# One plan for the whole recurrence and its tail, with constant matmuls in TensorE's gaps

## The chip, the cores and the metric

The kernel runs on one core of a Trainium2 chip. The metric is device time in microseconds of one execution, taken on the chip.

## What is computed

A linear-attention recurrence over 768 steps for 4 batches of 8 heads, with states of 40 x 40, then a mixture of 8 experts with a skip rule over the 3072 resulting rows of 320. Everything is float32.

```python
for t in range(S):
    y[:, :, t] = np.einsum('bhd,bhde->bhe', rt, state)
    Sa = np.einsum('bhde,bhe->bhd', state, at)
    state_decay = state * wt[:, :, None, :] - np.einsum('bhd,bhe->bhde', Sa, bt)
    state = state_decay + np.einsum('bhd,bhe->bhde', vt, kt)
...
do_compute = x @ w_skip > 0              # x: rows of y, 320 wide
e_idx = np.argmax(xc @ w_gate, axis=1)   # xc: the rows that compute
h = np.maximum(xc[mask] @ w1[e], 0.0)
y[mask] = gate_w[mask, None] * (h @ w2[e])
out[do_compute] = xc + y
```

## The kernel before

**The recurrence.** The 768 steps are cut into 24 chunks of 32 steps; heads and batches lie in 16 groups, and each chunk is worked in two halves `w` of 8 groups. A half passes through a chain: `ux` (TensorE product, pc<-R1t,L1t; a copy to UX), `uq` (product with the inverted triangle TB, four copies to R1t, and a mask product R1t<-R1t,mc, on GpSimd in all chunks but the last), `sst` (the state products, ps<-R1t,L2t, whose result goes to the next chunk's R1t and to YT). Every second chunk has `rs` (pc<-rrt,SS). Beside the chain stand work that prepares later chunks (`scan_z`, `scan_w`, `kbm`, `l1a`, `m1`, `kbt`, `m2`) and `tinv`, a long series of small VectorE products that inverts the triangle of four chunks at a time. `yt` turns a finished chunk, stores it and makes the scores; `route` picks each row's expert, ranks the rows with small matmuls by constants (pq<-oh,mc) and scatters them with GpSimd's indirect DMAs to the DRAM table xg.

**The order.** `Rec` records the calls of the engines as tasks instead of emitting them. `deps` finds what depends on what, `plan` is a list scheduler with fixed costs per operation (`cost`), a model of how TensorE's program is fetched, and PSUM banks that it hands out: PQ (1), PC (3) and PS (2), where a tile of the state products takes a PS bank only and PX (2) lies outside the plan. A task's priority is its place in the program less the length of the work that follows it (`up`). ScalarE's copies out of PSUM may go to VectorE where that starts more than `ALT` earlier. `flush` emits the tasks in planned order, so every recorded instruction carries line 255 in the profile, and one emitted directly carries line 129.

**The tail.** `flush` is called at the start of chunk 22. The tile M, which held work space of the earlier chunks, is then released, and its memory becomes WH0 and WL0, the high and low parts of expert 0's weights (made from WR by `split`: five casts and five subtractions, all on VectorE for expert 0), and a small tile ex. Chunks 22 and 23, the routing of the last rows and the following sums run in program order: `xacc` multiplies the rows already scattered for expert 0 (loaded back from xg by `early`) by the identity into PSUM, and `xadd` adds the rows of the last two chunks by one-hot matrices, so that expert 0 starts without waiting for their scatter. `warm(k)` puts k matmuls of constants (128 x 512) before some of these steps.

**The experts.** Eight experts follow, each with two layers of three products of split (fp32r) operands, weights loaded and split one expert ahead.

Of the kernel before, what the change touches and what calls it, by code (L numbers as in the profile page):

```python
# [43 lines left out]
class Task:  # L44
    __slots__=("e","op","calls","R","W","d","lat","out","p","n","pr","al","up","k","v","x","g")
class Eng:
# [15 lines left out]
class Rec:  # L62
# [4 lines left out]
    def __init__(s,nc):  # L67
        s.nc=nc; s.on=False; s.ni=0; s.tasks=[]; s.own={}; s.na=0; s.first={}; s.cache={}; s.banks={}; s.rest=()
        n=s.shim=Shim(); n.nc=nc
        for k,e in s.ENG.items(): setattr(n,k,Eng(s,e,getattr(nc,k)))  # L70
# [57 lines left out]
    def call(s,e,op,fn,a,k):  # L128
# [6 lines left out]
        r=[y for x in list(a[1:])+[v for n,v in k.items() if n!='accum_out'] for y in ap(x)]  # L135
        W=[u for x in w for u in s.use(x)]; R=[u for x in r for u in s.use(x)]
        d,lat=s.cost(e,op,w,r,a)
        own=dict(s.own)
        L=s.tasks[-1] if s.tasks else None
# [6 lines left out]
        t.x=s.pipe(w[0],r[0]) if op=='dma_start' else 0.0  # L146
        t.v=s.cost('V','copy',w,r,a)[0] if e=='A' and op=='copy' and 'PSUM' in str(r[0].space).upper() and W[0][0][0]=='s' else None
        s.tasks.append(t)
    def deps(s):
        acc={}  # L150
        for t in s.tasks: t.p,t.n,t.al=set(),[],set()
        for i,t in enumerate(s.tasks):
            for wr,L in ((0,t.R),(1,t.W)):
                u={}
                for n,q,m in L: u[n,q]=u.get((n,q),0)|m
                for (n,q),m in u.items():
                    if n[0]=='v': t.al.add(n[1])
                    h=acc.setdefault(n,[])
                    for j,w2,q2,m2 in h:
                        if j!=i and ((wr or w2) and q&q2 and m&m2 or n[0] in ('v','px') and s.tasks[j].e!=t.e and (n[0]!='v' or 'P' in (s.tasks[j].e,t.e))): t.p.add(j)  # L160
                    if wr and n[0] in 'sd': h[:]=[x for x in h if not (x[0]!=i and x[2]|q==q and x[3]|m==m)]
                    h.append((i,wr,q,m))
        for i,t in enumerate(s.tasks):
            for j in t.p: s.tasks[j].n.append(i)
        for t in reversed(s.tasks):
            t.up=t.d*s.PW+max([s.tasks[j].up+t.lat+t.x+(s.HOP if s.tasks[j].e!=t.e else 0) for j in t.n],default=0)
    def plan(s,keep=False):
# [8 lines left out]
        def put(i):  # L176
            pool[T[i].e].append(i)
            if T[i].v and not keep and s.ALT<9: pool['V'].append(i)
        for i in range(N):
            if not left[i]: put(i)  # L180
        nxt={e:0 for e in 'VAGPS'}; seq={e:[i for i in range(N) if T[i].e==e] for e in 'VAGPS'}
        def want(i):

            got={}; t0=0.0
            while old and old[0] in bank: old.pop(0)
# [9 lines left out]
        done=0; old=sorted(users); lv=lg=0.0  # L195
        while done<N:
            best=None
            for e in 'VAGPS':
# [6 lines left out]
                c.sort(key=lambda x:s.key[x[1]])  # L205
                x=c[0]; du=lambda i: T[i].v if e!=T[i].e else T[i].d
# [4 lines left out]
                if best is None or x[0]+(s.ALT if e!=T[x[1]].e else 0)<best[0]+(s.ALT if best[3]!=T[best[1]].e else 0): best=x+(e,)  # L211
# [4 lines left out]
            en[i]=e; st[i]=t0; fin[i]=t0+(t.v if e!=t.e else t.d)  # L216
            if e=='P':
# [21 lines left out]
        s.st,s.fin,s.bank_of,s.en,s.span=st,fin,bank,en,max(fin)  # L239
    LET=1.0; FAR=1.0; ALT=1.0; FILL=None  # L240
    def keys(s):
# [3 lines left out]
    def flush(s):  # L245
        s.on=False
        s.deps(); s.keys(); s.plan()
        def at(x,own):
            if isinstance(x,bass.AP) and x.name in s.banks:
                return bass.AP(s.banks[s.bank_of[own[x.name]]].tensor,x.offset,[tuple(d) for d in x.ap])  # L250
            return x
        work=[(s.st[i],i) for i in range(len(s.tasks))]+(s.fill() if s.FILL else [])
        for _,i in sorted(work,key=lambda x:x[0]):
            if isinstance(i,tuple): s.FILL(*i); continue
            for fn,a,k,own in s.tasks[i].calls: (fn if s.en[i]==s.tasks[i].e else s.nc.vector.tensor_copy)(*[at(x,own) for x in a],**{n:at(x,own) for n,x in k.items()})  # L255
        s.tasks=[]
    def fill(s):

        life={}
        for i,t in enumerate(s.tasks):  # L260
            for o in t.al:
                a,b=life.get(o,(1e9,0)); life[o]=(min(a,s.st[i]),max(b,s.fin[i]))
        P=sorted((s.st[i],s.fin[i]) for i in range(len(s.tasks)) if s.en[i]=='P')
        r=[]
        for (_,a),(b,_) in zip(P,P[1:]):
            if b-a<0.6: continue
            for n in s.banks:
                if all(e<a-0.3 or f>=b for o,(f,e) in life.items() if s.bank_of[o]==n):
                    r.append((a,(s.banks[n],min(512,int((b-a-0.2)*260))))); break
        s.nfill=r  # L270
        return r
class Ring:
# [13 lines left out]
ROUTE=('1c',('1c','3c'),('1c','3c'))  # L286
WT=(1,0,0,0,1)
def attn(ctx,tc,i,m,out,X):
# [15 lines left out]
    WR=m.WR  # L304
    mp=tc.tile_pool(name="M",bufs=1,side="right"); M=mp.__enter__().tile([128,13272],F32,name="M")
    off=[0]
# [216 lines left out]
    def uq(c,w):  # L523
# [7 lines left out]
        for g in (0,2,1,3):  # L531
            q,x=divmod(g,2); b=2*w+q
            A.copy(R1[x][c%NR1][uo[x]:uo[x]+32,4*b:4*b+4,:],UQ[32*g:32*g+32,:,:])
        L=c==NC-1
        for x in range(2):
            r=slice(64-64*x,128-64*x); o=R1[x][c%NR1][r,8*w:8*w+8,n-32:n]
            (V if L else G).tensor_tensor(o,o,mQ[r].unsqueeze(1).broadcast_to([64,8,32]),ALU.mult)
    YT,XS,SC={},{},{}
    def sst(c,w):
# [44 lines left out]
    if 1:  # L584

        with tc.manual_schedule(engines={ET.Pool}):
# [84 lines left out]
        for c in range(NC):  # L671
            ph,j=divmod(c,4)
            if c==20: m.load(0)
            if c==22:
                with tc.manual_schedule(engines={ET.Pool}): rec.flush()
                mp.__exit__(None,None,None)
                wp=m.ctx.enter_context(tc.tile_pool(name="mwa",bufs=1,side="right")); m.WA=[wp.tile([128,5632],F32,name=n) for n in ("WH0","WL0")]; ex=wp.tile([128,1408],F32,name="ex")
                tg=m.split(0)

# [94 lines left out]
        m.base_last()  # L774
        warm(WT[4]); m.xadd(pt,xl[:,1],1); m.pt0=pt; m.p2=p2
E_,CAP,FF,DM=8,256,1024,320
# [20 lines left out]
class Moe:  # L797
# [111 lines left out]
    def split(s,e,wp=None):  # L909
# [188 lines left out]
```

## Time and profile before

| | |
|---|---|
| Time, median of 3 runs | 656.82 us (650.41 to 658.1) |
| The profiled execution's own time | 658.57 us |
| Its span, first to last instruction | 656.8 us |
| Busy: TensorE, VectorE, ScalarE, GpSimd | 500.1, 489.9, 370.5, 283.8 us |
| Mean granted TensorE clock | 0.858 |
| TensorE matmul instructions | 10688 |

The rows below come from the trace of the profiled execution. Their times count from its first instruction. The granted clock is the share of TensorE's full speed that the chip granted in a stretch.

### The profile page before, as it was taken

The numbers are of one execution on the slowest core, as the hardware profiler recorded it, in microseconds if no ns is written. First come the engines' busy times: TensorE is split into PE (matmuls) and PEld (weight loads), VectorE is DVE, ScalarE is ACT, GpSimd is POOL, SyncE is SP. The second block draws the span as 40 slices with busy tenths as digits, with TensorE's granted clock in tenths as the row PEclk, the third lists the DMA queues.
The fourth block names the chain that finished last, engine by engine and source line by source line (L and its number), as shares of the span: only waits on it lengthen the run. The fifth ranks groups of instructions, "written<-read, shape, count | busy, mean of one in ns | idle before, by whom it ended". The sixth has DMA issues, their size and how long they took to land. (4 is left out here: it accounts for less than half of the span.)

```text
span 656.8 us, 25441 instructions
## 1 busy us (share of the span) xinstructions
PE 500.1 (76%) x10688; PEld 439.2 (67%) x10688; DVE 489.9 (75%) x1367; ACT 370.5 (56%) x890; POOL 283.8 (43%) x214
## 2 busy tenths in 40 slices
PE   0354368878787876867878978787766999999995
PEld 0343357766676766756767867676655599999995
DVE  8974849977986798696899777983672357888871
ACT  6244247765775766655885675775353055554440
POOL 5560244544545555236454532221311156666661
PEclk9999557878886898869896896887886699999999
DMA  7755762434542325234442535453242067776110
GB/s 218 203 142 140 213 202 44 121 103 113 158 128 71 113 82 155 74 98 118 132 126 82 144 78 127 133 170 108 59 130 73 21 187 227 225 223 212 52 49 24
DMA packets 74801, 83.34 MB, mean 127 GB/s; under 512 B 33598, under 2 KB 52619, under 8 KB 74680
## 3 DMA queue, kind: packets, MB, share of 16 engines
q1 hardware_dynamic: 72760, 77.85, 41.6%
q0 software_dynamic: 1920, 3.79, 1.6%
q8 instruction: 86, 1.41, 0.9%
q14 instruction: 35, 0.29, 0.1%
HBM read 70.75 MB, written 13.15 MB: 128 GB/s over the span
## 5 line engine op out<-in xcount | busy, mean ns | idle before, releaser
L255 POOL TENSOR_TENSOR R1t<-R1t,mc 64x256 f32<-64x256 f32 x86 | 67.9, 789 | 129.7 <-ACT R1t L255 66.8
L255 ACT COPY R1t<-pc 32x416 f32<-32x416 f32 (+3 forms) x251 | 95.6, 381 | 41.8 <-PE pc L255 35.4
L255 PE MATMUL ps<-R1t,L2t 128*40 128x104 f32 (+1 forms) x1376 | 84.3, 286 | 10.4 <-DVE YT L255 4.7
L255 PEld LDWEIGHTS ps<-R1t,L2t 128*40 128x40 f32 x1376 | 71.6, 143 | 18.2 <-issue 12.1
L255 DVE TENSOR_TENSOR px<-px,M 128x48 f32<-128x48 f32 (+24 forms) x240 | 59.8, 266 | 2.5
L129 POOL TENSOR_TENSOR WL<-WR,WH 128x1280 fp32r<-128x1280 f32 (+1 forms) x21 | 57.9, 2790 | 8.1 <-ACT WH L129 8.0
L255 POOL TENSOR_TENSOR WR<-WR,M 104x1024 f32<-104x1024 f32 x19 | 42.6, 2249 | 42.5 <-DVE M L255 21.6
L255 DVE TENSOR_TENSOR M<-M,px 128x48 f32<-128x48 f32 (+26 forms) x240 | 56.3, 253 | 2.7 <-ACT px L255 0.6
L255 ACT COPY R1t<-ps 40x288 f32<-40x288 f32 x88 | 34.6, 394 | 20.0 <-PE ps L255 18.3
L129 ACT CAST WH<-WR 128x1024 fp32r<-128x1024 f32 (+1 forms) x35 | 39.6, 1132 | 0.0
L255 DVE TENSOR_TENSOR R1t<-ps,D 40x160 f32<-40x160 f32 x84 | 26.9, 320 | 16.8 <-PE ps L255 14.6
L255 DVE TENSOR_TENSOR_SCAN M<-M 104x1041 f32<-104x1041 f32 (+1 forms) x15 | 39.0, 2597 | 0.1
L255 ACT COPY L2t<-pc 64x160 f32<-64x160 f32 x108 | 31.0, 287 | 13.5 <-PE pc L255 11.3
L255 PE MATMUL pc<-UX,TB 32*32 32x104 f32 (+1 forms) x1152 | 35.1, 267 | 3.6 <-issue 1.9
L129 DVE CAST ti<-xe 128x2 int32<-128x2 f32 x8 | 37.1, 4632 | 0.2
L129 POOL DMA_INDIRECT out<-ro,ti x16 | 16.2, 1013 | 46.4 <-DVE hL L129 12.5
L129 ACT ACTIVATE hH<-pc 128x512 fp32r<-128x512 f32 x21 | 12.6, 598 | 38.8 <-PE pc L129 32.9
L255 POOL DMA_INDIRECT xg<-XS,ix x20 | 20.3, 1017 | 28.7 <-DVE ix L255 7.5
L129 PE MATMUL pc<-xH,WH 128*128 128x256 f32 x126 | 32.5, 283 | 0.2 <-DVE hL L129 0.2
L255 PEld LDWEIGHTS pc<-UX,TB 32*32 32x32 f32 x1152 | 26.8, 121 | 8.1 <-issue 3.4
L129 DVE TENSOR_TENSOR WL<-WR,WH 128x1024 fp32r<-128x1024 f32 (+1 forms) x19 | 24.2, 1272 | 10.2 <-ACT WH L129 9.7
L255 PE MATMUL pc<-mc,WR 104*128 104x104 f32 x140 | 23.8, 310 | 8.2 <-ACT R1t L255 4.6
(285 smaller groups left out, 1410.1 us busy)
## 6 DMA issues: line engine op xcount, KB each, us to landing
WR<-w SPq DMA_DIRECT2D x16, 640.0 KB
WR<-kb SPq DMA_DIRECT2D x48, 208.0 KB
WR<-w SPq DMA_DIRECT2D x16, 512.0 KB
vvt<-vv SPq DMA_DIRECT2D x24, 208.0 KB
rrt<-rr SPq DMA_DIRECT2D x24, 208.0 KB
SCR<-vv SPq DMA_DIRECT2D x22, 208.0 KB
WR<-w SPq DMA_DIRECT2D x16, 256.0 KB
R1t<-vt SPq DMA_DIRECT2D x96, 40.0 KB
```

Of the source, the lines that this page charges most:

```text
L129: if not s.on: return fn(*a,**k)
L255: for fn,a,k,own in s.tasks[i].calls: (fn if s.en[i]==s.tasks[i].e else s.nc.vector.tensor_copy)(*[at(x,own) for x in a],**{n:at(x,own) fo ...
```

## The change

- The call of `flush` moves from the start of chunk 22 to the end of `attn`. All 24 chunks, the routing of the last rows, the split of expert 0's weights, `xacc` and `xadd` are recorded and planned as one. `warm` emits nothing while recording is on, so its matmuls go.
- M's release moves into the emission: the first task recorded after `gone` claims the whole of M in the dependencies, and when it is emitted, `swap` releases M and maps later uses to WH0, WL0 and ex.
- In the last two chunks the masks are recorded for VectorE and may go to GpSimd. Expert 0's split is cut into eleven pieces of 512 columns; casts may go to VectorE or ScalarE, subtractions to VectorE or GpSimd. For tasks from chunk 21 on, a move to another engine needs a gain of `ALT2` = 0.3 us, not 1.0.
- The accumulators of `xacc` and `xadd` are PX[1] and a tile of the PS banks, where they were two of the ring of the experts.
- The planner's TensorE costs change; the last free bank of a kind is kept for the oldest tile that has none; an accumulating matmul claims its whole bank; matmuls into PX with no successor count 10 us of work behind them.
- After planning, `replay` runs the order once more with somewhat longer VectorE and ScalarE costs, and `heat` looks at each gap between two TensorE tasks: where it is at least 0.35 us and the replayed busy share of some neighbouring stretch is under 0.62, it inserts a matmul of constants (`tri` by up to 510 columns of `mc`), up to 0.85 us long at the planner's cost, into a bank free by plan and replay, ahead of the next TensorE task, and repeats this while the conditions hold.

The core of the diff:

```diff
     def use(s,ap):
+        if n==s.home and s.gone==1: s.gone=2; return [(('s',n),15,(1<<13400)-1)]
...
-            if op=='transpose': return 0.144,0.2
-            return (0.0019*m if m>64 else 0.064 if m>40 else 0.008+0.00077*o if m==40 else 0.02 if m<32 else max(0.024,0.007+0.00034*o)),0.2
+            if op=='transpose': return 0.0925,0.2
+            return (0.01+0.00167*o if m>64 else max(0.057,0.008+0.00083*o) if m>40 else 0.003+0.00084*o if m>32 else max(0.0185,0.001+0.00042*o)),0.2
...
+        if e=='P' and k.get('start') is not k.get('stop'): W=[(n,15,(1<<512)-1) for n,q,f in W]
...
+        if s.flex:
+            n=int(np.prod([d[1] for d in w[0].ap[1:]]))
+            t.w=dict(A=0.17+0.00095*n,V=0.08+0.0006*n) if op in ('copy','tensor_copy') else dict(V=0.08+0.00107*n,G=0.2+0.0021*n)
+            t.d=t.w.pop(e)
...
-            t.up=t.d*s.PW+max([s.tasks[j].up+t.lat+t.x+(s.HOP if s.tasks[j].e!=t.e else 0) for j in t.n],default=0)
+            t.up=t.d*s.PW+max([s.tasks[j].up+t.lat+t.x+(s.HOP if s.tasks[j].e!=t.e else 0) for j in t.n],default=s.END if t.e=='P' and t.out[0]=='px' else 0)
...
+                g=s.first[o] in s.rest; q=old[g]
+                while q and q[0] in bank: q.pop(0)
+                if len(av)==1 and q[0]!=o: return None
...
+        if s.HEAT: s.heat()
+    END=10.0; ALT2=0.3; late=1e9; LET=1.0; FAR=1.0; ALT=1.0;
...
+            if isinstance(x,bass.AP) and x.name==s.home and own[None]:
+                s.new=s.new or s.swap()
...
+    HEAT=0.62; GAP=0.35; SLACK=0.15; FREE=0.3; HWIN=3.4; HT0=17.0; DRAIN=0.13; KV=1.08; KA=1.03; RAW=0.1
...
+    def heat(s):
+        T=s.tasks; rs,rf=s.replay(); life={}; real={}
...
+        for i,j in zip(P,P[1:]):
+            a,b=max(rf[i],s.HT0),rs[j]; key=s.st[j]; n=0
+            while b-a>=s.GAP and low(a,b)<s.HEAT:
+                best=None
+                for q,l in use.items():
+                    e=max([z for x,y,z in l if x<key],default=0.0)
+                    if e<=a-s.FREE and all(x>=key or y<=key for x,y,z in l) and (best is None or e<best[0]): best=(e,q)
+                if best is None: break
+                d=min(0.85,b-a-s.SLACK); c=int(d*600)
+                if c<64: break
...
+                t.calls=[(s.nc.tensor.matmul,(h[:,0:c],s.hot[0],s.hot[1][:,0:c]),dict(start=True,stop=True),{h.name:s.na,None:0})]
+                s.first[s.na]=q; s.bank_of[s.na]=q; T.append(t); s.st.append(key-1e-5+1e-7*n); s.fin.append(key); s.en.append('P')
+                add(a,a+d); a+=d+0.02; s.nheat+=d
...
+    def swap():
+        mp.__exit__(None,None,None)
+        wp=m.ctx.enter_context(tc.tile_pool(name="mwa",bufs=1,side="right")); m.WA=[wp.tile([128,5632],F32,name=n) for n in ("WH0","WL0")]; m.WH[0],m.WL[0]=m.WA
+        return [(0,m.WA[0]),(5632,m.WA[1]),(11264,wp.tile([128,1408],F32,name="ex"))]
...
-        L=c==NC-1
+        L=c>NC-3; rec.flex=L
...
-            m.consts()
+            m.consts(); rec.hot=(m.tri,m.mc[:,0:512])
...
-            if c==20: m.load(0)
-            if c==22:
-                with tc.manual_schedule(engines={ET.Pool}): rec.flush()
-                mp.__exit__(None,None,None)
...
-                tg=m.split(0)
+            if c==LATE-2: m.load(0)
+            if c==21: rec.late=len(rec.tasks)
+            if c==LATE: rec.gone=1; tg=m.split(0)
...
-        p2=[m.pr[0].tile([128,512],F32) for _ in range(2)]; pt=[p2[0][:,0:256],p2[0][:,256:512],p2[1][:,0:256]]
+        pz=ps_s.tile([128,256],F32); po=rec.own[pz.name]; pt=[PX[1][:,0:256],PX[1][:,256:512],pz]
...
-        warm(WT[4]); m.xadd(pt,xl[:,1],1); m.pt0=pt; m.p2=p2
+        warm(WT[4]); m.xadd(pt,xl[:,1],1)
+        with tc.manual_schedule(engines={ET.Pool}): rec.flush()
+        m.pt0=pt[:2]+[rec.banks[rec.bank_of[po]][:,0:256]]
...
-        cut=[(0,1024,V,128),(1024,2048,V,128),(2048,3072,G,128),(3072,4352,G,128),(4352,5632,G,128)]
+        cut=[(0,1024,V,128),(1024,2048,V,128),(2048,3072,G,128),(3072,4352,G,128),(4352,5632,G,128)] if e else [(q,q+512,V,128) for q in range(0,5632,512)]
```

## Rows read from the trace of the kernel before

**Rows 1.** Busy time by stretch of the span. Columns: stretch and its length in us; busy us and instructions of TensorE, its weight loads, VectorE, ScalarE and GpSimd; granted clock; DMA share; GB/s.

```profile
100.00:468.00 368.00, 295.66 (x7855) 252.51 (x7850) 293.22 (x1068) 247.15 (x652) 161.14 (x141) 0.84 0.39 111
435.60:468.00 32.40, 26.20 (x633) 22.22 (x632) 15.15 (x53) 19.99 (x54) 7.80 (x10) 0.84 0.38 106
468.00:488.00 20.00, 14.55 (x332) 12.27 (x328) 16.42 (x35) 8.04 (x21) 4.90 (x4) 0.83 0.39 110
488.00:510.00 22.00, 13.28 (x324) 10.88 (x324) 8.94 (x38) 9.55 (x25) 3.42 (x4) 0.71 0.28 88
510.00:523.50 13.50, 13.45 (x72) 7.86 (x72) 3.06 (x20) 1.02 (x4) 1.40 (x2) 0.58 0.06 18
523.50:639.00 115.50, 113.55 (x869) 111.64 (x868) 91.55 (x104) 59.41 (x80) 71.70 (x35) 1.00 0.55 168
```

**Rows 2.** The same view for the 22 stretches between 100 and 468 us, 84 us together, whose two-microsecond slices have a granted clock of at most 0.54: its line of sums.

```profile
sum 84.00, PE 76.93 PEld 67.43 DVE 57.48 ACT 42.65 POOL 34.64; mean PE 3.50 PEld 3.07 DVE 2.61 ACT 1.94 POOL 1.57
```

**Rows 3.** The same for the 21 stretches, 204 us together, whose slices have a granted clock of 0.99 or more.

```profile
sum 204.00, PE 158.02 PEld 133.35 DVE 169.24 ACT 153.39 POOL 90.69; mean PE 7.52 PEld 6.35 DVE 8.06 ACT 7.30 POOL 4.32
```

**Rows 4.** The timeline of TensorE from 254 to 270 us. Columns: start us, us, engine, line, operation, written from read, count, and in brackets the idle time before and what ended it.

```profile
257.58 0.22 PE L255 MATMUL pq<-rrt,vvt 104*64 104x64 f32 x1 [2.83 <-issue]
...
259.43 1.03 PE L255 MATMUL pq<-wx,YT 104*64 104x9 f32 x16 [1.13 <-ACT R1t L255]
...
265.80 2.15 PE L255 MATMUL ps<-R1t,L2t 128*40 128x72 f32 x32
```

**Rows 5.** The timeline of VectorE, around 267 us and from 470 to 516 us, same columns.

```profile
267.04 0.66 DVE L255 TENSOR_TENSOR R1t<-ps,D 40x160 f32<-40x160 f32 x2 [4.36 <-PE ps L255]
...
470.65 0.69 DVE L129 CAST WH<-WR 128x1024 fp32r<-128x1024 f32 x1
...
472.94 1.21 DVE L129 CAST WH<-WR 128x1024 fp32r<-128x1024 f32 x1
...
500.73 0.42 DVE L129 TENSOR_TENSOR R1t<-R1t,mc 64x256 f32<-64x256 f32 x1 [1.37 <-ACT R1t L129]
...
515.32 0.17 DVE L129 SCALAR_TENSOR_TENSOR oh<-px,oh 128x8 f32<-128x8 f32 x1
```

**Rows 6.** The timeline of TensorE again: the first product of `rs` (pc or pq<-rrt,SS) in chunks 10, 12, 20 and 22, which has one pair every second chunk, and one group of state products between.

```profile
251.44 1.09 PE L255 MATMUL pc<-rrt,SS 40*40 40x64 f32 x32
...
297.82 1.09 PE L255 MATMUL pq<-rrt,SS 40*40 40x64 f32 x32
...
435.62 1.09 PE L255 MATMUL pc<-rrt,SS 40*40 40x64 f32 x32
...
439.92 1.20 PE L255 MATMUL ps<-R1t,L2t 128*40 128x72 f32 x32
...
468.01 1.09 PE L129 MATMUL pc<-rrt,SS 40*40 40x64 f32 x32
```

**Rows 7.** The timeline of ScalarE in the tail.

```profile
471.68 0.51 ACT L129 COPY UX<-pc 128x416 f32<-128x416 f32 x1 [0.27 <-PE pc L129]
...
480.76 2.04 ACT L129 COPY R1t<-pc 32x416 f32<-32x416 f32 x4
...
485.68 0.80 ACT L129 COPY R1t<-ps 40x288 f32<-40x288 f32 x2 [2.88 <-PE ps L129]
```

**Rows 8.** The timeline of TensorE in the tail. ps<-mc is the constant matmul `warm`, one matmul counted as two instructions; pc<-mc,ex and the first pc<-ex,XS are the sums for expert 0, pq<-oh,mc is a rank matmul.

```profile
473.65 2.02 PE L129 MATMUL ps<-R1t,L2t 128*40 128x72 f32 x29 [1.34 <-POOL R1t L129]
...
479.40 0.92 PE L129 MATMUL pc<-UX,TB 32*32 32x104 f32 x32
...
486.96 1.00 PE L129 MATMUL pc<-R1t,L1t 128*32 128x104 f32 x32
...
508.44 1.28 PE L129 MATMUL ps<-R1t,L2t 128*40 128x32 f32 x30 [0.47 <-DVE R1t L129]
...
510.05 2.07 PE L129 MATMUL ps<-mc 128*128 128x512 f32 x2 [0.34 <-DVE YT L129]
...
513.71 3.63 PE L129 MATMUL pc<-mc,ex 128*128 128x128 f32 x16
...
517.27 3.12 PE L129 MATMUL pc<-ex,XS 128*128 128x256 f32 x8
...
520.32 0.40 PE L129 MATMUL pq<-oh,mc 128*32 128x8 f32 x16
...
520.65 1.44 PE L129 MATMUL ps<-mc 128*128 128x512 f32 x2
```

**Rows 9.** The timeline of GpSimd in the tail: masks (R1t<-R1t,mc) and scatters of rows to DRAM (xg).

```profile
470.68 2.92 POOL L129 TENSOR_TENSOR R1t<-R1t,mc 64x256 f32<-64x256 f32 x2 [7.53 <-ACT R1t L129]
...
492.08 0.72 POOL L129 TENSOR_TENSOR R1t<-R1t,mc 64x256 f32<-64x256 f32 x1 [8.10 <-ACT R1t L129]
...
493.99 1.01 POOL L129 DMA_INDIRECT xg<-XS,ix  x1 [0.16 <-POOL R1t L129]
...
496.57 0.97 POOL L129 DMA_INDIRECT xg<-XS,ix  x1 [1.57 <-DMA xg<-XS,ix]
```

**Rows 10.** Groups of VectorE's instructions from 468 to 523.5 us: line, engine, operation, written from read, shapes, count, busy us and mean ns, idle time before. These two are the split of expert 0's weights.

```profile
L129 DVE TENSOR_TENSOR WL<-WR,WH 128x1024 fp32r<-128x1024 f32 (+1 forms) x5 | 7.0, 1409 | 0.1
...
L129 DVE CAST WH<-WR 128x1024 fp32r<-128x1024 f32 (+1 forms) x5 | 4.2, 848 | 0.1
```

**Rows 11.** The timeline of SyncE's queue: the load of expert 0's rows from xg.

```profile
499.77 0.42 SPq L129 DMA_DIRECT2D ex<-xg  x1
```

More of the change, by code (lines that the diff above doesn't have):

```diff
@@ L44 @@
 class Task:
-    __slots__=("e","op","calls","R","W","d","lat","out","p","n","pr","al","up","k","v","x","g")
+    __slots__=("e","op","calls","R","W","d","lat","out","p","n","pr","al","up","k","v","x","g","w")
 class Eng:
@@ L67, in __init__ @@
     def __init__(s,nc):
-        s.nc=nc; s.on=False; s.ni=0; s.tasks=[]; s.own={}; s.na=0; s.first={}; s.cache={}; s.banks={}; s.rest=()
+        s.nc=nc; s.on=False; s.ni=0; s.tasks=[]; s.own={}; s.na=0; s.first={}; s.cache={}; s.banks={}; s.rest=(); s.home=None; s.flex=0; s.gone=0; s.new=None
         n=s.shim=Shim(); n.nc=nc
@@ L135, in call @@
         r=[y for x in list(a[1:])+[v for n,v in k.items() if n!='accum_out'] for y in ap(x)]
-        W=[u for x in w for u in s.use(x)]; R=[u for x in r for u in s.use(x)]
+        W=[u for x in w for u in s.use(x)]
+        if e=='P' and k.get('start') is not k.get('stop'): W=[(n,15,(1<<512)-1) for n,q,f in W]
+        R=[u for x in r for u in s.use(x)]
         d,lat=s.cost(e,op,w,r,a)
-        own=dict(s.own)
+        own=dict(s.own); own[None]=s.gone
         L=s.tasks[-1] if s.tasks else None
@@ L147, in call @@
         t.v=s.cost('V','copy',w,r,a)[0] if e=='A' and op=='copy' and 'PSUM' in str(r[0].space).upper() and W[0][0][0]=='s' else None
+        t.w={}
+        if t.v: t.w['V']=t.v
+        if s.flex:
+            n=int(np.prod([d[1] for d in w[0].ap[1:]]))
+            t.w=dict(A=0.17+0.00095*n,V=0.08+0.0006*n) if op in ('copy','tensor_copy') else dict(V=0.08+0.00107*n,G=0.2+0.0021*n)
+            t.d=t.w.pop(e)
         s.tasks.append(t)
@@ L177, in put @@
             pool[T[i].e].append(i)
-            if T[i].v and not keep and s.ALT<9: pool['V'].append(i)
+            if not keep and s.ALT<9:
+                for f in T[i].w: pool[f].append(i)
         for i in range(N):
@@ L184, in want @@
             got={}; t0=0.0
-            while old and old[0] in bank: old.pop(0)
             for o in T[i].al:
@@ L194, in plan @@
         pos=s.POS0; blk=0; got=0.0; dq=0.0; track=[(0,0.0)]
-        done=0; old=sorted(users); lv=lg=0.0
+        done=0; old=[[o for o in sorted(users) if (s.first[o] in s.rest)==g] for g in (False,True)]; lv=lg=0.0
         while done<N:
@@ L205, in plan @@
                 c.sort(key=lambda x:s.key[x[1]])
-                x=c[0]; du=lambda i: T[i].v if e!=T[i].e else T[i].d
+                x=c[0]; du=lambda i: T[i].w[e] if e!=T[i].e else T[i].d
                 while True:
@@ L210, in plan @@
                     x=f[0]
-                if best is None or x[0]+(s.ALT if e!=T[x[1]].e else 0)<best[0]+(s.ALT if best[3]!=T[best[1]].e else 0): best=x+(e,)
+                alt=lambda y,f: y[0]+((s.ALT if y[1]<s.late else s.ALT2) if f!=T[y[1]].e else 0)
+                if best is None or alt(x,e)<alt(best,best[3]): best=x+(e,)
             assert best, "no task can start"
@@ L215, in plan @@
                 bank[o]=k; at[k]=None
-            en[i]=e; st[i]=t0; fin[i]=t0+(t.v if e!=t.e else t.d)
+            en[i]=e; st[i]=t0; fin[i]=t0+(t.w[e] if e!=t.e else t.d)
             if e=='P':
@@ L239, in plan @@
         s.st,s.fin,s.bank_of,s.en,s.span=st,fin,bank,en,max(fin)
-    LET=1.0; FAR=1.0; ALT=1.0; FILL=None
+        if s.HEAT: s.heat()
+    END=10.0; ALT2=0.3; late=1e9; LET=1.0; FAR=1.0; ALT=1.0;
     def keys(s):
@@ L248, in at @@
         def at(x,own):
+            if isinstance(x,bass.AP) and x.name==s.home and own[None]:
+                s.new=s.new or s.swap()
+                p,f=divmod(x.offset,x.ap[0][0]); o,t=max(((o,t) for o,t in s.new if o<=f),key=lambda y:y[0])
+                st=t.ap[0][0]; y=bass.AP(t.tensor,t.offset+p*st+f-o,[(st,x.ap[0][1])]+[tuple(d) for d in x.ap[1:]])
+                return y if x.dtype==F32 else y.bitcast(x.dtype)
             if isinstance(x,bass.AP) and x.name in s.banks:
@@ L251, in at @@
             return x
-        work=[(s.st[i],i) for i in range(len(s.tasks))]+(s.fill() if s.FILL else [])
+        work=[(s.st[i],i) for i in range(len(s.tasks))]
         for _,i in sorted(work,key=lambda x:x[0]):
-            if isinstance(i,tuple): s.FILL(*i); continue
-            for fn,a,k,own in s.tasks[i].calls: (fn if s.en[i]==s.tasks[i].e else s.nc.vector.tensor_copy)(*[at(x,own) for x in a],**{n:at(x,own) for n,x in k.items()})
+            for fn,a,k,own in s.tasks[i].calls: (fn if s.en[i]==s.tasks[i].e else s.nc.scalar.copy if s.en[i]=='A' else s.nc.vector.tensor_copy if 'copy' in s.tasks[i].op else s.nc.gpsimd.tensor_tensor)(*[at(x,own) for x in a],**{n:at(x,own) for n,x in k.items()})
@@ L256, in flush, with replay @@
         s.tasks=[]
-    def fill(s):
-        life={}
-        for i,t in enumerate(s.tasks):
+    HEAT=0.62; GAP=0.35; SLACK=0.15; FREE=0.3; HWIN=3.4; HT0=17.0; DRAIN=0.13; KV=1.08; KA=1.03; RAW=0.1
+    def replay(s):
+        T=s.tasks; N=len(T); O=sorted(range(N),key=lambda i:(s.st[i],i)); own={}; hand={}
+        for i in O:
+            for o in T[i].al: own.setdefault(s.bank_of[o],[]).append((o,i))
+        for n,l in own.items():
+            seq=[]
+            for o,i in l:
+                if not seq or seq[-1][0]!=o: seq.append((o,[]))
+                seq[-1][1].append(i)
+            for (_,a),(_,b) in zip(seq,seq[1:]):
+                for i in b: hand.setdefault(i,[]).extend(a)
+        st=[0.0]*N; fin=[0.0]*N; land=[0.0]*N; free=dict.fromkeys('VAGPS',0.0); prev={}
+        pos=s.POS0; blk=0; got=0.0; dq=0.0; track=[(0,0.0)]; lv=lg=0.0
+        for i in O:
+            t=T[i]; e=s.en[i]; x=free[e]
+            for j in list(t.p)+hand.get(i,[]): x=max(x,land[j]+(s.HOP if s.en[j]!=e or 'dma' in T[j].op else 0))
+            if e=='V':
+                if t.g: x=max(x,lg-0.14)
+                if prev.get(e) in t.p: x+=s.RAW
+            if e=='G': x=max(x,lv-0.14)
+            d=(t.w[e] if e!=t.e else t.d)*(s.KV if e=='V' else s.KA if e=='A' else 1)
+            st[i]=x; fin[i]=x+d
+            if e=='P':
+                n=t.k
+                while n>0:
+                    m=min(n,max(0,256*(blk+1+s.OFF)-pos)); x+=d/t.k*m; pos+=m; n-=m
+                    track.append((pos,x))
+                    if n>0:
+                        while track[0][0]<256*(blk+s.PHI): track.pop(0)
+                        got=max(track[0][1],got)+s.FETCH; x=max(x,got+s.LAND); blk+=1
+                        track.append((pos,x))
+                fin[i]=x
+            if t.g and e=='V': lv=fin[i]
+            if e=='G': lg=fin[i]
+            free[e]=fin[i]; prev[e]=i; lat=t.lat if e in 'PS' or 'dma' in t.op else 0
+            if t.x: dq=max(dq,fin[i]+1.0)+t.x; lat=max(lat+t.x,dq+1.2-fin[i])
+            land[i]=fin[i]+lat
+        return st,fin
@@ L261, in fill @@
+    def heat(s):
+        T=s.tasks; rs,rf=s.replay(); life={}; real={}
+        for i,t in enumerate(T):
             for o in t.al:
                 a,b=life.get(o,(1e9,0)); life[o]=(min(a,s.st[i]),max(b,s.fin[i]))
[L263 to L269, printed above, removed]
@@ L270, in fill, with add @@
-        s.nfill=r
-        return r
+                real[o]=max(real.get(o,0),rf[i])
+        use={n:sorted(life[o]+(real[o],) for o in life if s.bank_of[o]==n) for n in s.banks}
+        P=sorted((i for i in range(len(T)) if s.en[i]=='P'),key=lambda i:(s.st[i],i))
+        last=rf[P[-1]]; step=0.1; busy=np.zeros(int(last/step)+60)
+        def add(a,b):
+            k=int(a/step)
+            while k*step<b:
+                busy[k]+=max(0,min(b,(k+1)*step)-max(a,k*step)); k+=1
+        for i,j in zip(P,P[1:]+P[-1:]): add(rs[i],max(rf[i],min(rs[j],rf[i]+s.DRAIN)))
@@ new lines, in heat, with low @@
+        W=int(s.HWIN/step)
+        def low(a,b):
+            k0=max(0,int(a/step)-W); c=np.concatenate([[0],np.cumsum(busy[k0:int(b/step)+W+1])]); w=(c[W:]-c[:-W])/(W*step)
+            return w.min()
+        s.nheat=0.0
+        for i,j in zip(P,P[1:]):
[8 more added lines that the diff above has]
+                if c<64: break
+                q=best[1]; s.na+=1; t=Task(); n+=1
+                t.e,t.op,t.W,t.R,t.d,t.lat,t.out,t.p,t.n,t.al,t.up,t.k,t.x,t.v,t.w,t.g=('P','heat',[],[],d,0.2,('v',s.na),set(),[],{s.na},0,4,0.0,None,{},False)
+                h=next(iter(s.banks.values()))
+                t.calls=[(s.nc.tensor.matmul,(h[:,0:c],s.hot[0],s.hot[1][:,0:c]),dict(start=True,stop=True),{h.name:s.na,None:0})]
+                s.first[s.na]=q; s.bank_of[s.na]=q; T.append(t); s.st.append(key-1e-5+1e-7*n); s.fin.append(key); s.en.append('P')
+                add(a,a+d); a+=d+0.02; s.nheat+=d
@@ L286 @@
 ROUTE=('1c',('1c','3c'),('1c','3c'))
-WT=(1,0,0,0,1)
+WT=(1,0,0,0,1); LATE=22
 def attn(ctx,tc,i,m,out,X):
@@ L304, in attn @@
     WR=m.WR
-    mp=tc.tile_pool(name="M",bufs=1,side="right"); M=mp.__enter__().tile([128,13272],F32,name="M")
+    mp=tc.tile_pool(name="M",bufs=1,side="right"); M=mp.__enter__().tile([128,13272],F32,name="M"); m.WA=[M[:,0:5632],M[:,5632:11264]]; ex=M[:,11264:12672]
+    def swap():
+        mp.__exit__(None,None,None)
+        wp=m.ctx.enter_context(tc.tile_pool(name="mwa",bufs=1,side="right")); m.WA=[wp.tile([128,5632],F32,name=n) for n in ("WH0","WL0")]; m.WH[0],m.WL[0]=m.WA
+        return [(0,m.WA[0]),(5632,m.WA[1]),(11264,wp.tile([128,1408],F32,name="ex"))]
+    rec.home,rec.swap=M.name,swap
     off=[0]
@@ L537, in uq @@
             (V if L else G).tensor_tensor(o,o,mQ[r].unsqueeze(1).broadcast_to([64,8,32]),ALU.mult)
+        rec.flex=0
     YT,XS,SC={},{},{}
@@ L672, in attn @@
             ph,j=divmod(c,4)
-            if c==20: m.load(0)
-            if c==22:
-                with tc.manual_schedule(engines={ET.Pool}): rec.flush()
-                mp.__exit__(None,None,None)
-                wp=m.ctx.enter_context(tc.tile_pool(name="mwa",bufs=1,side="right")); m.WA=[wp.tile([128,5632],F32,name=n) for n in ("WH0","WL0")]; ex=wp.tile([128,1408],F32,name="ex")
-                tg=m.split(0)
+            if c==LATE-2: m.load(0)
+            if c==21: rec.late=len(rec.tasks)
+            if c==LATE: rec.gone=1; tg=m.split(0)
             if c: rs(c,0)
@@ L916, in split @@
         s.WH[e],s.WL[e]=h,l
-        cut=[(0,1024,V,128),(1024,2048,V,128),(2048,3072,G,128),(3072,4352,G,128),(4352,5632,G,128)]
+        cut=[(0,1024,V,128),(1024,2048,V,128),(2048,3072,G,128),(3072,4352,G,128),(4352,5632,G,128)] if e else [(q,q+512,V,128) for q in range(0,5632,512)]
         for a,b,E,pe in cut:
-            s.top(A if e else V,h[:,a:b],r[:,a:b])
-            if e==0: yield
-            s.low(E if e else V,l[:pe,a:b],r[:pe,a:b],h[:pe,a:b]); yield
+            s.rec.flex=s.rec.on; s.top(A if e else V,h[:,a:b],r[:,a:b])
+            s.low(E if e else V,l[:pe,a:b],r[:pe,a:b],h[:pe,a:b]); s.rec.flex=0; yield
     def R(s,t): return t.bitcast(mybir.dt.float32r)
```

## The prediction

> **What bounds the kernel now.** I read the stages first: busy time of each engine and granted clock by stretch [rows 1]. Three regimes stand there. From 523.5 us on the experts keep TensorE busy for 113.55 of 115.50 us at full clock; nothing in the change touches that work, so it is carried over as it is. From 100 to 468 us runs the part whose order the planner wrote (chunks up to 21): no engine is full, VectorE has 293 and TensorE 296 of 368 us, and the granted clock is 0.84. From 468 to 523.5 us runs the tail in program order (chunks 22 and 23, routing of the last rows, the sums that prepare expert 0): TensorE 41.3 of 55.5 us, VectorE 28.4, with the clock falling to 0.83, 0.71 and 0.58.
>
> The clock first. With the two levels 1.2 and 2.4 GHz, a mean of 0.84 over 368 us means 2 x 0.16 x 368, some 118 us, at the lower one. In 22 stretches that lie wholly near it, 84 us together, TensorE is busy 76.9 us and VectorE 57.5, 68% [rows 2]; in 21 stretches at full clock VectorE reaches 169 of 204 us, 83% [rows 3]. So VectorE, the other engine near the limit, starves when TensorE is slow. One case shows how it goes: TensorE stops 2.83 us at "issue" and 1.13 us for a ScalarE copy, comes back at half speed, and takes 2.15 us for a state product of 32 instructions [rows 4]; VectorE waits 4.36 us for it [rows 5]. At 439.92 a group of the same size and shape took 1.20 us [rows 6].
>
> Then the tail. Two chunks in the planner's order took 468.01 - 435.62 = 32.4 us [rows 6]; chunks 22 and 23, with less work, took from 468 to 510, 42 us. The rows show program order as the reason: the copy of UX for half 0 of chunk 22 ends at 472.2 [rows 7], but its product with TB starts at 479.40, since the state products of the other half (473.65, held up by GpSimd's mask) and more stand ahead of it [rows 8].
>
> **Part by part.** The sum is made against the profiled execution's 658.57 us (span 656.80 and 1.77 outside it), which is 1.75 above the median of 656.82.
>
> Chunks 22 and 23 in the planner's order. TensorE is busy 27.8 us between 468 and 510 [rows 1]. From 435.6 to 468 the planned order kept TensorE busy for 26.2 of 32.4 us, 81% [rows 1]. At that share the 27.8 us need 34 us. At full clock the same work is about 14.55 x 0.83 + 13.28 x 0.71 = 21.5 us, which at 81% need 26. The chain of one half is no shorter than some 20 us, an estimate: three passes (the end of chunk 21, 22, 23) of two products and a state product at 0.9, 0.9 and 1.3 us [rows 8], a copy of UX at 0.5, four copies at 2.0 together and two at 0.8 [rows 7] and a mask at 0.4 [rows 5], 6.8 us each. I take 32, near the upper value, because the clock is not safe there: minus 10 (bounds minus 16 and 0; nothing is gained if the chain through copies, masks and state products, and not the order, sets the pace).
>
> The masks of these chunks may go to VectorE: one takes 0.42 us there [rows 5], 0.72 on GpSimd alone, and 2.92 for two while VectorE splits weights [rows 9]. A cast there took 1.21 us beside the mask, its twin just before 0.69 [rows 5]. The new flexible split may put some subtractions on GpSimd, where they meet such pairs again. By the Trainium skill ("SBUF — State Buffer", section "SBUF: two separate sides") VectorE and GpSimd share a port pair that one holds for its whole instruction; these rows agree. The split costs VectorE 7.0 + 4.2 = 11.2 us [rows 10], beside 27 us in which it idles in the tail [rows 1], and expert 0 needs it only at the end; so I cost its new cut into eleven pieces at nothing, and if that cover is gone at up to 11.
>
> The end, 510 to 523.5. The two constant matmuls called warm go: the first holds the transposes from 510.05 for 1.9 us, the second hides behind the one-hot. The chosen expert of the last chunk is known at 515.49 [rows 5] but its rank matmul starts at 520.32, behind the sums for expert 0 (3.63 and 3.12 us) [rows 8]: 4.8 us. A planner that puts these sums into earlier gaps saves both, 6.7 us; I take 6.5 (bounds minus 9 with full clock, minus 2). The lower one holds if the sums can't come earlier: they read rows loaded from DRAM behind two scatters of GpSimd, at 493.99 and 496.57, which wait for each other, and the load is issued at 499.77 [rows 9, 11]. In the new order the scatters need not stand behind the masks, which is why I don't take the bound. The queue of SyncE gets the tail's stores and loads in planned order; the load of expert 1's weights is needed only after expert 0's eighth of the 133 us from there to the end, so I cost it at nothing, up to plus 3 if it slips.
>
> Fillers and replanned body, 0 to 468. If all 118 us at low clock ran with VectorE at 83% rather than 68%, they would take 118 x 0.68/0.83, 97 us: a gain of 21 at most. I count half, minus 11, since some drops begin at stops like the one at "issue", in which a filler can't run either. Against it stands their price. TensorE idles 72 us in the body [rows 1]. The nearest row to a filler is a warm matmul: its pair took 2.07 us at half clock and 1.44 across a rise [rows 8], where the planner counts at most 0.85. A filler stands in TensorE's in-order queue ahead of the next real product, and behind the release of its bank by ScalarE or VectorE; whoever waits for that product (a copy, a mask, the next state product) gets its delay too. If fillers fill half of the idle time, some 36 us at planned cost, and a fifth falls where real work was ready, that is plus 7. Net minus 4, bounds minus 20 (clock held, nothing on the path) and plus 30 (no clock won, four in five parts of 36 us on the path). Each filler also lengthens TensorE's program by four instructions, which moves all later stops at "issue" against the plan; the new costs of transposes and the rule that keeps the last free bank for the oldest tile change the order as well. I give these 5 us either way, inside the bounds.
>
> Sum: 658.6 - 10 - 6.5 - 4 = 638.1 for a profiled execution, 636.3 beside the median; I say 637.
>
> **The rivals.** First, the fillers hold the clock. For it: the low stretches are many and short (22, of 2 to 8 us), each behind a gap of TensorE. Body minus 20, chunks minus 15, end minus 7: 657 - 42 = 615; I allow 610 to 625. Against it: the gaps come from a replay at fixed costs, while the trace's pace varies from 32.4 us for two chunks to 46.4 (251.44 to 297.82) [rows 6].
>
> Second, the change does little of what it says: gaps that the replay sees are not the gaps of the chip, or no bank is free, the clock stays at 0.84, and the tail gains only its end and a little: 657 - 8 = 649 (644 to 660). The stop of 2.83 us at "issue" speaks for it [rows 4]. The Trainium skill ("TensorE: Matmul & The Clock Gate", section "A second HAM failure mode: psum-queue depth-cycling") tells of a kernel whose clock oscillated because TensorE paused often between groups in rotating banks; fillers with pauses between them would be the same picture, and the time that of this rival. No run here shows it yet.
>
> Third, slower: fillers become the bound. At half clock a filler lasts twice what was planned, TensorE is already at 76.9 of 84 us there [rows 2], so each filler in such a stretch pushes real work, the gaps slide, and the next filler is misplaced too. It decides when the fillers' time on the path, beyond what clock they win, passes 16.5 us, the tail's gain: 100 fillers of 0.5 us planned are some 100 us at half speed; a third on the path gives plus 33, and 657 - 16.5 + 33 = 673 (662 to 690).
>
> **How the numbers follow.** Forecast 0.43 (626 to 648, most of it below 644), clock held 0.15, little done 0.20, fillers bind 0.22. Two per cent, about what a measurement of this kernel can tell, is 13 us: 643.7 and 670. Faster: 0.15 + 0.38 = 0.53. Slower: 0.15, two thirds of the last rival, and 0.03 for a plan that falls badly: 0.18. Same: 0.29. The range, 616 to 671, leaves out half of the first rival and the upper part of the last.
>
> **What would show it.** Right: the start of the experts moves from 523.5 to about 503, with their 133 us unchanged; no warm pair at the end, the sums for expert 0 ahead of the last chunk's transposes; the last rank matmul within 1 us of its expert choice; 512-column products of the constant table scattered over the body, a mean clock there above 0.90, and VectorE's share above 0.80. Wrong: a clock unchanged beside many fillers; TensorE's busy share up with waits of VectorE and ScalarE for TensorE longer; a tail still above 50 us, waiting for scatter or bank; a slower expert stage, which I hold to be untouched.

## The result and the profile after

The changed kernel takes 621.35 us (median of 4, 618.27 to 627.3) where the kernel before took 654.04 beside it; the ratio is 0.951, with an interval from 0.941 to 0.961. Medians are of all executions; a ratio and its interval leave out those more than 1.5% above the fastest of their kernel. The forecast was 637 us in a range from 616 to 671: faster, as said, but by 33 us where some 20 were forecast.

The profiled execution took 618.27 us (span 616.5), 40.3 less than that of before. That one lies high among the executions of before and this one is the lowest of its four, so the differences below add up to some 8 us more than the 33 us of the medians. The page's row of granted clock, in 40 slices:

```profile
PEclk9999996888989997998889899989869999999998
```

Busy time by stretch, cut at the same places of the program as [rows 1]: the planned body, chunks 22 and 23 in two parts with the end, and the experts (columns as there).

```profile
100.00:424.00 324.00, 273.85 (x7491) 225.72 (x7488) 285.07 (x1037) 230.71 (x610) 157.96 (x133) 0.92 0.42 120
424.00:444.50 20.50, 18.02 (x467) 15.05 (x466) 16.94 (x54) 14.29 (x37) 8.93 (x10) 0.92 0.47 143
444.50:465.00 20.50, 17.80 (x364) 14.57 (x362) 13.62 (x45) 11.38 (x29) 8.20 (x8) 0.75 0.53 133
465.00:485.30 20.30, 17.39 (x336) 11.74 (x335) 10.30 (x49) 7.05 (x20) 2.90 (x3) 1.00 0.20 63
485.30:600.00 114.70, 114.25 (x879) 112.83 (x880) 89.94 (x105) 59.43 (x81) 70.67 (x34) 1.00 0.55 168
```

The three marks of the sum are the first product of `rs` in chunk 22, the end of the last state products and the experts' first product. Before they stand at 468.01 [rows 6], at 510 and at 523.5 us. After, in the timeline of TensorE (planned instructions are line 273 now, others 130):

```profile
444.51 1.09 PE L273 MATMUL pc<-rrt,SS 40*40 40x64 f32 x32
...
476.72 0.80 PE L273 MATMUL ps<-R1t,L2t 128*40 128x32 f32 x32
...
485.29 0.38 PE L130 MATMUL pc<-xH,WH 128*128 128x256 f32 x1
```

So the body is 23.5 us shorter, the two chunks take 33.0 us for 42 (9.0 less), the end 7.8 for 13.5 (5.7 less), and the experts to the end of the span 131.2 for 133.3. Both tail terms came out near the 10 and 6.5 us of the forecast. The body, forecast at 4 with 20 as the most, holds the surprise.

The sums over stretches with a low clock and with a full one, as in [rows 2] and [rows 3], now from 100 to 432 us, where the body of before runs to 468:

```profile
sum 30.00, PE 28.98 PEld 24.28 DVE 26.21 ACT 15.49 POOL 15.76; mean PE 2.63 PEld 2.21 DVE 2.38 ACT 1.41 POOL 1.43
...
sum 256.00, PE 209.54 PEld 170.63 DVE 230.71 ACT 188.70 POOL 117.04; mean PE 17.46 PEld 14.22 DVE 19.23 ACT 15.72 POOL 9.75
```

The reader is to see two things. Stretches near the lower clock add up to 30 us in place of 84. But VectorE is also busier where the clock is full: 230.7 of 256 us, 90%, where [rows 3] give 83%. In a stretch at full clock it isn't the clock that holds VectorE back, so this hints at a better order. It doesn't prove one, since the stretches don't hold the same work.

### The profile page after: what moved, and what is told of

Its sections match the earlier page's. It is cut to its first block, busy times and chain, and to the rows that moved or that the text cites. A ratio compares the mean times of both kernels' runs of the same rounds, so it can differ in the third digit from the quotient of the medians.

```text
span 616.5 us, 25741 instructions
## 1 busy us (share of the span) xinstructions
PE 519.2 (84%) x10840; PEld 429.7 (70%) x10840; DVE 483.1 (78%) x1390; ACT 366.8 (59%) x876; POOL 294.3 (48%) x217
## 4 chain that ended last, share of the span: by engine, by line
PE 48%; DVE 30%; issue 9%; DMA 4%; ACT 4%; POOL 3%; SPq 0%; POOLq 0%; DVEq 0%; ACTq 0%
PE pc L273 18%; PE ps L273 12%; DVE M L273 8%; DVE R1t L273 7%; DVE px L273 7%; PE pc L130 5%; PE px L130 5%; PE pq L273 5%; PE ps L130 3%; ACT R1t L273 2%; DMA out<-ro,ti 2%; DVE YT L273 2%; POOL WR L273 1%; POOL R1t L273 1%; DVE L2t L273 1%
## 5 line engine op out<-in xcount | busy, mean ns | idle before, releaser
L273 POOL TENSOR_TENSOR R1t<-R1t,mc 64x256 f32<-64x256 f32 x89 | 73.5, 826 | 137.4 <-ACT R1t L273 67.0
L273 ACT COPY R1t<-pc 32x288 f32<-32x288 f32 (+3 forms) x290 | 110.5, 381 | 38.1 <-PE pc L273 31.1
L273 PE MATMUL ps<-R1t,L2t 128*40 128x104 f32 (+2 forms) x1536 | 82.4, 261 | 13.4 <-DVE YT L273 6.1
L273 DVE TENSOR_TENSOR M<-M,px 128x48 f32<-128x48 f32 (+22 forms) x240 | 57.1, 253 | 3.8 <-ACT px L273 1.5
L273 PE MATMUL ps<-mc 128*128 128x510 f32 (+14 forms) x136 | 60.0, 558 | 0.0
L273 POOL DMA_INDIRECT xg<-XS,ix x24 | 25.7, 1070 | 46.9 <-DVE YT L273 11.9
L273 PE MATMUL pc<-UX,TB 32*32 32x72 f32 (+1 forms) x1280 | 37.6, 261 | 7.5 <-DVE base L273 2.3
L273 DVE TENSOR_TENSOR_SCAN M<-M 104x1041 f32<-104x1041 f32 (+1 forms) x15 | 35.7, 2381 | 0.2
L273 PEld LDWEIGHTS ps<-mc 128*128 128x128 f32 x136 | 23.3, 194 | 16.4 <-issue 14.9
L273 ACT COPY L2t<-pc 64x160 f32<-64x160 f32 x95 | 27.2, 287 | 10.4 <-PE pc L273 8.7
```

## The experiments

All ratios are against the kernel before on the same chip; before had a median of 656.46, 658.46 and 657.55 us in the three sets.

**Without fillers.** Theory A said that the fillers held the clock and so shortened the body; its rival B, that the edits of the planner did.

```diff
-    HEAT=0.62; GAP=0.35; ...
+    HEAT=0; GAP=0.35; ...
```

> The changed kernel without any filler; plan, tail and costs as changed. Theory A (the fillers hold the clock and that made chunks 2 to 21 some 22 us shorter): the body loses its gain, about 641 us, granted clock 0.86 again. Theory B (the planner's new TensorE costs and bank rule gave a better order, fillers do little): 620 to 625 us, and a clock that is lower with no loss of time.

Measured: 629.46 us (621.56 to 632.23). The body keeps most of its gain without a filler: chunk 22 begins at 450.16 us, 17.9 of the 23.5 us earlier than before (at 446.10 in a later execution of the same kernel).

```profile
450.16 1.09 PE L273 MATMUL pc<-rrt,SS 40*40 40x64 f32 x32
```

A falls as the main cause, though the time itself, 629, lies between A's 641 and the 620 to 625 of B. The clock is no lower than before for that: 0.86 from 110 to 440 us, where before has 0.84.

**The tail in program order again, with and without fillers.** The order is written out at the start of chunk 22 and the edits to the tail are taken back; the second kernel has no fillers besides.

```diff
-            if c==LATE: rec.gone=1; tg=m.split(0)
+            if c==22:
+                with tc.manual_schedule(engines={ET.Pool}): rec.flush()
+                mp.__exit__(None,None,None)
...
+                tg=m.split(0)
```

> The changed planner with its fillers, but the order is written out at the start of chunk 22 and the tail runs in program order, as in the kernel before. Theory A and theory B alike: the body keeps its gain of some 22 us and the tail takes 55 us again, so about 635 us. If it is 650 or more, the body's gain came from planning past chunk 22 (theory C: a longer view gives the late chunks better priorities).

> As the run before, and without fillers: of the change only the new costs, the bank rule and the wider claim of accumulating matmuls are left. Theory A: the time of the kernel before, 650 to 658 us. Theory B: about 635 us.

Measured: 646.22 us (ratio 0.985, from 0.979 to 0.992) with fillers and 641.49 (0.979, from 0.967 to 0.991) without. Both miss theory B's 635, by 11 and by 6 us, and the second lies below A's 650 to 658 as well. The tail's worth can be read from marks: from the first product of `rs` in chunk 22 to the experts' first product, 55.0 and 56.5 us in these two kernels, 40.0 in the one above, so some 16 us. What is left of the change without tail and fillers, costs and bank rules, is worth some 14 by its ratio. In this order the fillers bring nothing that can be seen: chunks 2 to 22 take 343.8 us with them and 342.0 without, although the clock from 110 to 440 us rises from 0.87 to 0.90. Theory C, that the longer view of the plan made the body faster, falls as its main cause too: chunk 22 begins at 452.0 us in the kernel whose plan ends there (first two rows, no fillers; the third row is of the kernel above, with the tail in the plan).

```profile
452.00 1.09 PE L130 MATMUL pc<-rrt,SS 40*40 40x64 f32 x32
...
508.48 0.39 PE L130 MATMUL px<-xH,WH 128*128 128x256 f32 x1
```

```profile
490.14 0.39 PE L130 MATMUL pc<-xH,WH 128*128 128x256 f32 x1
```

**Fillers of 64 columns.**

```diff
-...(h[:,0:c],s.hot[0],s.hot[1][:,0:c])...
+...(h[:,0:64],s.hot[0],s.hot[1][:,0:64])...
```

> The changed kernel with every filler at its place, with its waits and its four instructions, but 64 columns long where it was up to 510. Theory A: too little work to hold the clock, so nearly the time without fillers, 632 to 641 us. Theory B, or a gain by the shift of TensorE's instruction fetches: 617 to 623 us.

Measured: 624.27 us (0.954, from 0.937 to 0.970), clock 0.89 from 110 to 440 us. It lies between the runs with and without fillers, and its interval holds both; by itself it settles neither what the fillers are worth nor whether their columns or their places bring it. It lies below theory A's 632 to 641, though the upper end of its interval, 637, reaches into it.

**Which edit of the planner?** There is no run of the new costs alone, without the bank rule. Tried were the bank rule alone and the old cost of transposes in the changed planner, and beside them two controls whose edit means nothing: the cost of a handover between engines at 0.09 us in the kernel before, and in the changed planner.

```diff
 # bank rule alone, in the kernel before
+                g=s.first[o] in s.rest; q=old[g]
+                while q and q[0] in bank: q.pop(0)
+                if len(av)==1 and q[0]!=o: return None
...
 # control, in the kernel before (and the same in the changed planner)
-    HOP=0.08; PW=1.25; ...
+    HOP=0.09; PW=1.25; ...
...
 # old transposes, in the changed planner
-            if op=='transpose': return 0.0925,0.2
+            if op=='transpose': return 0.144,0.2
```

> The kernel before with one edit: the last free bank of a kind is kept for the oldest tile without one. Theory B1 (the bank rule made the body faster): about 641 us, as with all planner edits and nothing else. Theory B2 (the new TensorE costs did): the time of the kernel before, 650 to 660 us. Theory D (the body's gain is the scatter of a plan that any small edit redraws): anywhere between 640 and 665.

> A control: the kernel before with the planner's cost of a handover between engines at 0.09 us, where it was 0.08; nothing else. Theories B1 and B2: within 6 us of the kernel before. Theory D: the order is redrawn and the time moves by 8 us or more, either way.

> The same control on the changed planner: all planner edits, no fillers, order written out at chunk 22, and the handover at 0.09 us. Theories B1 and B2: within 6 us of 641. Theory D: it moves by 8 us or more, either way.

> All planner edits, no fillers, order written out at chunk 22, but a transpose costs 0.144 us in the plan as before, not 0.0925. If the gain sits in the cheaper transposes (part of theory B2): back towards 655 us. If it sits in the bank rule (B1): 641 us. Theory D: anywhere from 635 to 660.

| kernel, tail in program order, no fillers | us | ratio, interval |
|---|---|---|
| all planner edits (above) | 641.49 | 0.979, 0.967 to 0.991 |
| bank rule alone | 645.23 | 0.982, 0.973 to 0.992 |
| before, handover 0.09 | 640.46 | 0.977, 0.970 to 0.985 |
| all planner edits, handover 0.09 | 639.90 | 0.977, 0.968 to 0.986 |
| all planner edits, transposes 0.144 | 648.16 | 0.985, 0.974 to 0.996 |

The first control decides. A hundredth of a microsecond in one constant of the kernel before changes only the order and, with it, who makes some copies out of PSUM (on balance ten go from VectorE to ScalarE). It brings 15 us by its ratio and 18 by the medians, as much as all edits of the planner together. So neither edit can be given credit of its own, and B1 and B2 fall. D did not come as written either: the second control was to move by 8 us or more and moved by 1.6. What the runs show is that each of the five new orders is faster than that of before, by 10 to 15 us by their ratios, 13 in the mean; their medians lie between 640 and 648 us, that of before at 656 to 658. The moved copies don't explain it: VectorE has 1355 to 1383 instructions in the five, and 1367 in before. The chunk 22 of before begins at 468.01 [rows 6], that of the control at 450.6:

```profile
450.59 1.09 PE L129 MATMUL pc<-rrt,SS 40*40 40x64 f32 x32
```

Busy time from 110 to 440 us, first before, then the control (columns as [rows 1]):

```profile
110.00:440.00 330.00, 265.62 (x7082) 226.92 (x7080) 272.51 (x981) 222.76 (x591) 149.93 (x129) 0.84 0.40 113
```

```profile
110.00:440.00 330.00, 259.50 (x7269) 221.94 (x7268) 277.01 (x997) 231.14 (x620) 150.32 (x130) 0.87 0.42 117
```

In the same 330 us VectorE has done 4.5 us more work and ScalarE 8.4 us more, and TensorE has been busy 6.1 us less at a clock of 0.87 for 0.84. The gain is uneven: before, the five groups of four chunks from chunk 2 on take 65.6, 75.0, 83.8, 68.4 and 64.4 us between their first products of `rs`; in the control 71.5, 65.8, 76.8, 70.4 and 58.6. Three groups are faster and two slower. Which feature of the old order makes it slow was not found.

**The fillers, in two orders.** The changed kernel and the same without fillers, and both once more with the handover at 0.09, so that the order is another one.

> The changed kernel once more, beside the next three on one chip. So far: 621 us with fillers, 629 without and 624 with fillers of 64 columns, each from few executions that spread over 10 us. If the fillers' columns (the clock) bring the difference: again some 8 us below the run without fillers, and in the second pair too. If not: within 3 us in both pairs, or of opposite sign.

> The changed kernel without fillers, same plan. Fillers worth something: 627 to 631 us. Worth nothing: within 3 us of the run with fillers.

> The changed kernel with the handover at 0.09 us in the plan: a second draw of the order, with the fillers that a replay of this order asks for. As a control on the whole change: if an order is worth what this planner gives on average, 615 to 630 us. Fillers worth something: some 8 us below the next run.

> The same second draw without fillers. Fillers worth something: 8 us above the run before. Worth nothing: within 3 us.

| | with fillers | without |
|---|---|---|
| order of the change | 622.28, ratio 0.949 (0.941 to 0.956) | 627.93, ratio 0.958 (0.952 to 0.964) |
| order with handover 0.09 | 620.13, ratio 0.948 (0.942 to 0.954) | 628.14, ratio 0.960 (0.954 to 0.966) |

The fillers bring 5.7 and 8.0 us, the same sign in both; in the third order, with the tail in program order, they brought none. The changed kernel's redraw, 620.13, is no other time than its own: with the tail in the plan both orders give 628 without fillers. The best kernel run is this redraw, within the scatter of the changed one.

What the fillers do in the body, with the order of the change, first without them:

```profile
110.00:440.00 330.00, 270.32 (x7436) 231.14 (x7432) 287.00 (x1036) 231.05 (x612) 156.33 (x135) 0.87 0.43 120
```

```profile
110.00:440.00 330.00, 280.35 (x7563) 229.37 (x7562) 289.45 (x1048) 234.13 (x620) 159.18 (x137) 0.92 0.43 121
```

The clock rises from 0.87 to 0.92. With the two levels of 1.2 and 2.4 GHz that is 2 x 0.05 x 330, 33 us less at the lower one. VectorE gets 2.5 us more done in the same time, and chunks 2 to 22 take 330.6 us for 334.0 (336.5 for 343.1 in the other order). These are single executions: the same kernel without fillers took 339.4 us there in the first experiment. Whether it is the clock that brings the 5.7 and 8.0 us is not shown, since in the third order the clock rose and the time did not fall.

## Why the prediction was right and wrong

**The tail, right.** Forecast 16.5 us. The marks show 14.7; the experiments 16 by the marks (56.5 to 40.0 us) and 14 by the ratios (0.979 to 0.958), both without fillers. The sums for expert 0 did not move where I put them: they still follow the last chunk's transposes. But the rank matmul starts 0.18 us after VectorE has chosen the expert (480.66), where it waited 4.8 us before.

```profile
480.49 0.17 DVE L273 SCALAR_TENSOR_TENSOR oh<-px,oh 128x8 f32<-128x8 f32 x1
```

```profile
478.90 0.63 PE L273 MATMUL px<-mc,ex 128*128 128x128 f32 x4
...
480.47 0.44 PE L273 MATMUL ps<-mc,ex 128*64 128x128 f32 x4
480.84 0.31 PE L273 MATMUL pc<-oh,mc 128*32 128x8 f32 x16
...
482.14 0.65 PE L273 MATMUL ps<-ex,XS 128*64 128x256 f32 x4
482.72 1.12 PE L273 MATMUL pc<-mc 128*128 128x510 f32 x2
483.68 1.03 PE L273 MATMUL px<-ex,XS 128*128 128x256 f32 x4
```

The sums (px<-mc,ex and ps<-mc,ex) fill the time in which VectorE chooses. The bound that I set aside, scatters that wait for each other ahead of the load, is there, but no row shows the sums waiting for it: the load is issued at 471.42, the sums start at 478.90.

```profile
463.54 1.01 POOL L273 DMA_INDIRECT xg<-XS,ix  x1 [3.41 <-DVE ix L273]
468.13 0.97 POOL L273 DMA_INDIRECT xg<-XS,ix  x1 [3.58 <-DMA xg<-XS,ix]
```

The last row but one of TensorE's is a filler on the path: the sums ahead of it end at 482.8, and the last ones start at 483.68, some 0.9 us later, behind the filler. That is the price that the forecast feared, met here once; the body was not searched for more.

The planned tail holds a wait that the forecast did not have. The chain that ended last shows it (start, us, what), and below it the mask in GpSimd's timeline:

```profile
441.42 0.73 POOL R1t L273
442.32 5.82 DMA xg<-XS,ix
...
449.10 0.73 POOL R1t L273
```

```profile
448.30 1.51 POOL L273 TENSOR_TENSOR R1t<-R1t,mc 64x256 f32<-64x256 f32 x2 [4.97 <-DMA xg<-XS,ix]
```

A mask stands behind a scatter in GpSimd's queue and starts only when the scatter's rows have landed, after 4.97 us of waiting; the forecast named this queue only for the scatters' own delay. Such waits are not new: masks waited for scatters five times in each kernel, 13.1 us in all before and 18.3 us now.

**Fillers, right in net size, wrong in their parts.** The forecast took 11 us of clock gain and 7 of price. Its rate was 21 us for 118 us at the low clock; the 33 us that the fillers took off give 5.9 by that rate, beside 5.7 and 8.0 measured in two orders and none in a third. So less of the low clock was removed than half, and the price was small: of the 78 fillers 47 stand before 84 us, yet chunk 2 begins only 0.3 to 2.6 us later than in the runs without. The fillers keep TensorE busy for 71 us, yet its busy time grows by only 34.5 us (519.2 for 484.7 without), because its other instructions take less time:

```profile
L273 PE MATMUL ps<-mc 128*128 128x510 f32 (+14 forms) x136 | 60.0, 558 | 0.0
...
L273 PE MATMUL pc<-mc 128*128 128x510 f32 (+2 forms) x20 | 11.2, 677 | 0.0
```

The rival in which the fillers become the bound had its arithmetic right and its premise wrong: a filler of 510 columns, a pair of instructions, takes 0.89 us in a row of seven at a clock of 1.00 (below), not the 1.44 to 2.07 of [rows 8], which were taken at 0.77 and 0.50.

```profile
71.49 6.25 PE L273 MATMUL ps<-mc 128*128 128x510 f32 x14
```

**The redrawn order, wrong.** The step that failed is "I give these 5 us either way". Each of the five new orders, by whatever edit, was worth 10 to 15 us, 13 in the mean. The old order was slow; why stays open. With 13 in place of 0 the sum reads 658.6 - 10 - 6.5 - 4 - 13 = 625, beside a measured 618 to 627. That the time still fell inside the stated range is in part luck: its lower part was put there for the clock of the first rival, not for another order. Nor did the rows used give a hint of it. The forecast reads 32.4 us for two chunks and 46.4 for two others [rows 6] as a varying pace, but the work differs: VectorE is busy 15.1 us in the first pair [rows 1] and 37.5 in the other, and after the change the same pairs still take 27.2 and 37.7 us.

**The rivals.** "The fillers hold the clock" gave the time best (610 to 625), and for the wrong reason: it put 20 us on the clock in the body, where fillers and clock together bring at most the 5.7 to 8.0 us of the pairs, and the order the larger part. "Little of what it says" fell with the clock in the body, 0.92 for 0.87 in the pairs above; the picture of the Trainium skill that it leaned on ("TensorE: Matmul & The Clock Gate", section "A second HAM failure mode: psum-queue depth-cycling"), a clock that swings because of pauses between groups, is not what these fillers brought from 110 to 440 us.

## What to carry to other kernels

Before an edit to a planner is given credit, redraw the plan with an edit that means nothing and measure it: here the redraw alone was worth as much as the edit to the costs and rules. Redraw the changed plan too: here that moved nothing (641 and 640 us, 628 and 628), so one slow order stood behind the gain and not a wide scatter of all orders. Constant matmuls in TensorE's waiting time brought 1% in two orders and nothing in a third; they are the last step, after the order.

## What the runs showed of the hardware

The granted clock of a whole run can't be set beside that of another here. The profile gives 1.00 from 60 to 70 us both without fillers (first row below) and with them (second row), but the same product takes 1.93 us in one and 1.10 in the other. With fillers it takes 1.93 us too at 95.85 us, where the profile gives 0.50. So the 1.00 of the run without fillers was no full clock. The mean of before also goes from 0.855 to 0.905 over the eleven executions in the set of the two orders. From 110 us on, where the text above compares clocks, clock and duration go together, as in the state products of 2.15 us at 0.50 [rows 4] and 1.20 us at 1.00 [rows 6].

```profile
67.18 1.93 PE L273 MATMUL pc<-WR,L1t 40*32 40x64 f32 x64 [1.25 <-ACT R1t L273]
```

```profile
67.78 1.10 PE L273 MATMUL pc<-WR,L1t 40*32 40x64 f32 x64
```

A faster TensorE brought little here. Before chunk 2 it took 1.10 us in place of 1.93 for the product above, and chunk 2 began no earlier. In the body 33 us less at half speed went with 3.4 and 6.6 us in two pairs of executions, and in the third order 0.03 more clock went with nothing.
